# The opening of an attention-and-experts kernel: rest rows loaded per head pair, one load order over two queues, own buffers per pair, seven first banks

## The chip, the cores and the metric

The kernel runs on one core of one Trainium2 chip. The metric is the device time of one execution in microseconds (us); the value of a kernel is the median of its runs. Five engines work side by side, each through its own queue in order: PE (TensorE, matrix products and transposes), ACT (ScalarE: exp, relu, copies), DVE (VectorE: elementwise work), POOL (GpSimd) and SP (SyncE), the last two mostly issuing loads and stores. An engine whose next instruction waits holds up everything behind it. PSUM is the matrix results' memory, eight banks of 128 x 512 fp32.

## What is computed

```python
def phi(x):
    return np.where(x > 0, x, np.exp(x) - 1.0) + 1.0
q_p, k_p = (phi(q), phi(k))                      # q, k, v: 8 batches, 8 heads, 576 rows, 64
kv = np.einsum('bhsd,bhse->bhde', k_p, v)
z = np.sum(k_p, axis=2)
num = np.einsum('bhsd,bhde->bhse', q_p, kv)
den = np.einsum('bhsd,bhd->bhs', q_p, z)[..., None] + 1e-06
attn = num / den                                 # -> x: 4608 rows, 512 columns
p = domain_probs / (domain_probs.sum(-1, keepdims=True) + 1e-09)
for e in range(E):                               # 4 experts, w1 512 x 1024, w2 1024 x 512
    h = np.maximum(x @ w1[e], 0.0)
    out += p[:, e:e + 1] * (h @ w2[e])
```

Linear attention per head, then a mixture of four two-layer experts with the weights p.

## The kernel before

Each batch of 576 rows is cut into 512 main rows (NT) and 64 *rest rows* (R). The 512 columns of x are four head pairs of 128 columns (pr = 0 to 3; also the four pieces dc of the first layer's contraction). The kernel goes through three stages.

*Opening.* Batch 0 goes through attention on PE with transposes done by PE, in `attention(..., two=True)`: exp of k and q on ACT (L472), phi on DVE (L456, L457), transposes of q (L484), kv products (L515, L517, L523), copies of kv and of transposed q on ACT (L534, L535, L497), numerator and denominator (L548, L550), division on DVE (L555, L556), and `turn_x`, which transposes x back (L671) and copies it into xt0 (L676). Then expert 0 runs on x of batch 0: `first_l1` (matmuls L681, relu L713 on ACT) and `first_l2` (L691; sum on DVE, L748 and L750), followed by experts 1 to 3 on the same rows. Attention of batch 1 (kv products L520 and L523, transposes L484 and L489, numerators L571) is woven in between. Where PE would stand idle early, `keep_warm` puts in matmuls whose result nobody reads (L1075).

*Steady part.* From about 81 us, 64 units (`l1_seven` L835, `l2_unit` L911) run a seven-product scheme over the remaining row blocks and experts, with sums of weights that DVE forms beforehand (`sums_w1` L633, `sums_w2` L654; buffers w1x and t123), and attention of batches 2 to 7 with transposes by DMA.

*End.* The last unit's sums and stores.

The order on each queue comes from a planner written into the kernel (`Plan`): every operation is added with engine, estimated duration, priority and the keys that it reads and writes; `lay_out` places the operations in time, `deadlines` sets the priority of all but PE's work to the latest time that PE's plan allows, and a second `lay_out` gives the order in which they are issued. POOL's queue keeps the order in which operations were added. T0 is the planned time of the first unit, TU the planned length of one; WARM and COLD set where filler matmuls are put.

Loads (`dma`, all at L262) go through SP's queue or POOL's. POOL's loads can convert fp32 to fp16 on the way. POOL waits for the landing of the load eight before it in its own row, so that at most eight are under way. In the opening, `load_pair` brings k, q, v of a head pair (main rows, 256 KB each; v through POOL in fp16), `load_rest` the 64 rest rows of all heads of k, v or q (128 KB, runs of 256 bytes, over 64 partitions). The order before: SP: k0, rest k, q0, rest v, v0. POOL, from the landing of k0 on (hold="k0"): k1 q1 v1, k2 q2 v2, k3 q3 v3, the four pieces of w1 of expert 0, probabilities, four pieces of w2 of expert 0, rest q, w1 and w2 of expert 1, then k, v, q of batch 1's first pair and its rest rows, weights of expert 2, and so on.

Pair 3 reuses the load buffers of pair 0; kqp, ek and the transpose bank (l2b1) alternate over two or are shared. The rest rows' phi and the cast of v run over all heads at once (L379, L382, L374, L375) and every kv product ends with one matmul over them (L523). `first_l1(0, ..., 4)` starts four of the eight column blocks (fj) of the first layer in four PSUM banks, dc by dc; the others follow in three banks, four matmuls each.

Of the kernel before, what the change touches and what calls it, by code (L numbers as in the profile page):

```python
# [20 lines left out]
class Plan:  # L21
# [13 lines left out]
    def __init__(self):  # L35
        self.ops = []
        self.wr = {}
        self.rd = {}

    def add(self, eng, dur, pri, fn, r=(), w=(), move=0.0, after=0.0, lead=1.2):  # L40
        n = len(self.ops)
        deps = set()
        for key in r:
            if key in self.wr:
                deps.add(self.wr[key])
            self.rd.setdefault(key, []).append(n)
# [12 lines left out]
    def deadlines(self):  # L59
# [10 lines left out]
        for n, o in enumerate(ops):  # L70
            if o["eng"] != "PE" and o["pri"] >= -99:
                o["pri"] = late[n]
# [61 lines left out]
def kernel(  # L134
# [27 lines left out]
    WARM, COLD = 22.0, 28  # L162
    T0, TU = 79.0, 6.4
# [7 lines left out]
    def sb(name, shape, dt):  # L171
# [47 lines left out]
    v00 = vss[1].rearrange("p h c d -> p (h c d)").bitcast(FP16)[:, 2 * C * D :].rearrange(  # L219
        "p (h c d) -> p h c d", h=2, c=C  # L220
    )
    ones = sb("ones", [P, 2, 1], FP16)
    rc4 = sb("rc4", [P, 2 * C], FP32)
# [20 lines left out]
    def lk(i):  # L244

        return ("l2b2k", "l2b2n") if i == 2 else ("l2b%d" % i,)

    def stage_keys(i):

        if i < 2:  # L250
            return ("st", i, 0), ("st", i, 1), ("st", i, 2)
        return ("xp", 0), ("xp", 1), ("u2", 0)
# [35 lines left out]
    def v16(i):  # L288

        flat = vss[i].rearrange("p h c d -> p (h c d)").bitcast(FP16)  # L290
        return flat[:, 0 : 2 * C * D].rearrange("p (h c d) -> p h c d", h=2, c=C)

    def load_pair(b, pr, queue, pri, after=0.0, hold=None):
        hs = slice(2 * pr, 2 * pr + 2)
        n = 3 if b < 2 else 2
        i = rot("stage%d" % n, n) if n == 2 else rot("stage3", 3)
        stage[b, pr] = i
        kk = stage_keys(i)
        vo = vss[i] if b or queue == "SP" else v16(i)
        parts = [(k, kqs[i][:, 0], kk[0]), (v, vo, kk[2]), (q, kqs[i][:, 1], kk[1])]  # L300
        if b == 0:
            parts[1:] = parts[:0:-1]
        for t, o, key in parts:
            if (b, pr, key) == (0, 0, kk[1]):
                load_rest(0, "SP", 0, parts=(0,))
            keys = (key, "v00") if (b, key) == (1, ("st", 1, 2)) else (key,)
            dma(queue, pri, o, t[b, hs, 0:NT].rearrange("h (p c) d -> p h c d", c=C), keys,
                0.7,
                hold="w" if b == 2 else hold if key == kk[0] else None,
                mark="k0" if (b, pr, key) == (0, 0, kk[0]) else None, after=after)  # L310

    def load_rest(b, queue, pri, after=0.0, parts=(0, 1, 2)):
        par = b % 2
        rs = slice(par * R, par * R + R)
        for i in parts:
            t, o = ((k, kqr[rs, 0]), (v, vr[rs]), (q, kqr[rs, 1]))[i]
            dma(queue, pri, o, t[b, :, NT:S].rearrange("h s d -> s h d"), (("str", par, i),),
                1.1,
                hold="w" if b in (2, 3) else None, after=after)
# [26 lines left out]
    def probs(b0, b1, raw, keys, out_key, pri):  # L346
# [7 lines left out]
            r=keys, w=(out_key,))  # L354
# [10 lines left out]
    def rest_maps(b, pe_mode, pri, parts=(0, 1)):  # L365
# [19 lines left out]
        if not pe_mode:  # L385
            pl.add("SP", 1.25, pri + 1, lambda: nc.sync.dma_start_transpose(
                out=qTr[par][:, :, rs], in_=kqpr[rs, 1].rearrange("p h d -> p (h d)")),
                r=("qpr",), w=[("qTr", par, i) for i in range(DC)], move=0.9, lead=0.2)

# [44 lines left out]
    def attention(b, pr, pe_mode, pri, step, two=False):  # L434
# [16 lines left out]
        zi = pr if two else rot("kvz", 2)  # L451
# [8 lines left out]
        if two:  # L460
            vh = v00 if pr == 0 else v16(si)
            vk = "v00" if pr == 0 else sk[2]

        def vcast():
            if two:
                nc.scalar.copy(vh, vs)
            else:
                nc.scalar.copy(vp[:, :, :, 0:D].rearrange("p c h d -> p h c d"), vs)

        order_ = (0, 1)  # L470
        for i in order_:
# [4 lines left out]
            if i == 0 and not (two and pr):  # L476
                pl.add("ACT", 0.52, pri + step, vcast, r=(sk[2],), w=(vk,))
        if pe_mode:

            tq, tk = (l2b[1].bitcast(FP16), "l2b1") if two else (tbank, "l2b3")  # L480

            def turn():
# [4 lines left out]
                if two:  # L487
                    return
# [7 lines left out]
                   r=(("kqp", pi, 1), "ident") + (() if two else ("qpr",)), w=(tk,))  # L496
            pl.add("ACT", 0.5, pri + 3.5 * step, lambda: nc.scalar.copy(  # L497
                qT.rearrange("p c t -> p (c t)"), tq[:, 0:NT]), r=(tk,), w=(("qT", ti),))
            if not two:
                pl.add("DVE", 0.2, pri + 3.5 * step, lambda: nc.vector.tensor_copy(  # L500
                    qTr[par][:, pr, rs], tq[:, NT : NT + R]), r=(tk,), w=(("qTr", par, pr),))
# [6 lines left out]
        if two:  # L508
            kvs_, kvk = l2b[2][:, 0 : 2 * DE], ("l2b2k",)
        kv3 = kvs_.rearrange("p (h e) -> p h e", h=2)  # L510

        def kv():
            for c in range(C):
                if two:
                    nc.tensor.matmul(out=kv3[:, :, 0:D], lhsT=kp[:, c], rhs=vh[:, :, c],  # L515
                                     start=(c == 0), stop=False, skip_group_check=True)
                    nc.tensor.matmul(out=kv3[:, :, D:DE], lhsT=kp[:, c], rhs=ones,  # L517
                                     start=False, stop=False, skip_group_check=True)
                else:
                    nc.tensor.matmul(  # L520
                        out=kvs_, lhsT=kp[:, c], rhs=vp[:, c], start=(c == 0), stop=False
                    )
# [6 lines left out]
                skip_group_check=two,  # L529
# [7 lines left out]
        pl.add("PE", 0.42 if two else 0.3, pri + 4 * step, kv,  # L537
# [4 lines left out]

        if two:
            den = l2b[2][:, 256 : 256 + 2 * C].rearrange("p (c h) -> p c h", h=2)

            def nd0():
                for c in range(C):
# [590 lines left out]
```

## Time and profile before

| | |
|---|---|
| median of 10 runs | 498.7 us (498.3 to 499.67) |
| profiled execution | 499.45 us, of which the span from first to last instruction is 497.2 |
| mean granted clock of PE | 0.999 |
| DMA traffic | 67.11 MB, 135 GB/s in the mean; read from HBM 45.16 MB |
| chain that ended last | PE 88%, DMA 6%, ACT 2% |
| costliest lines | L835 and L911, the two layers of the steady part: 40% and 38% of the chain |

Read it so: PE is busy nearly from end to end, and the chain that ended last runs through PE for most of the span; the rest of that chain lies in the opening.

Landings that the text uses (issue by the timeline, plus time to landing from the view of DMA issues):

| load | issued | landed |
|---|---|---|
| k0 (SP) | 0.74 | 3.7 |
| v3 (POOL) | 9.95 | 14.75 |
| w1 of expert 0, first piece | 10.66 | 17.2 |
| probabilities, 16 KB | 12.78 | 22.3 |
| w1 of expert 1, last piece | 23.72 | 32.6 |
| batch 1, first pair: k, v, q | 29.46, 30.66, 31.92 | 39.3, 40.5, 41.5 |

### The profile page before, as it was taken

The numbers are of one execution on the slowest core, as the hardware profiler recorded it, in microseconds if no ns is written. First come the engines' busy times: TensorE is split into PE (matmuls) and PEld (weight loads), VectorE is DVE, ScalarE is ACT, GpSimd is POOL, SyncE is SP. The second block draws the span as 40 slices with busy tenths as digits, with TensorE's granted clock in tenths as the row PEclk, the third lists the DMA queues.
The fourth block names the chain that finished last, engine by engine and source line by source line (L and its number), as shares of the span: only waits on it lengthen the run. The fifth ranks groups of instructions, "written<-read, shape, count | busy, mean of one in ns | idle before, by whom it ended". The sixth has DMA issues, their size and how long they took to land.

```text
span 497.2 us, 15010 instructions
## 1 busy us (share of the span) xinstructions
PE 486.2 (98%) x6109; PEld 431.0 (87%) x6109; DVE 408.9 (82%) x1033; ACT 366.5 (74%) x690; POOL 41.6 (8%) x67
## 2 busy tenths in 40 slices
PE   7899999999999999999999999999999999999995
PEld 5644456999999999999999999999999999999995
DVE  5688998988998999899988899889988675767664
ACT  5637758978987798769876988689766767676641
POOL 7566700000000000000000000000000000000000
PEclk9999999999999999999999999999999999999999
DMA  8999979846674774775755755755623333423211
GB/s 228 197 235 213 264 153 212 198 108 171 124 167 120 165 175 125 124 176 118 167 130 158 146 149 123 172 136 121 161 54 86 35 97 44 77 54 86 45 44 42
DMA packets 125573, 67.11 MB, mean 135 GB/s; under 512 B 95520, under 2 KB 119600, under 8 KB 125504
## 3 DMA queue, kind: packets, MB, share of 16 engines
q1 hardware_dynamic: 116112, 51.79, 47.1%
q0 software_dynamic: 9232, 14.10, 13.8%
q8 instruction: 47, 0.77, 0.6%
q10 hardware_dynamic: 160, 0.26, 0.1%
q14 instruction: 22, 0.18, 0.1%
HBM read 45.16 MB, written 9.44 MB: 110 GB/s over the span
## 4 chain that ended last, share of the span: by engine, by line
PE 88%; DMA 6%; ACT 2%; DVE 1%; POOL 1%; issue 1%; SPq 0%; DVEq 0%; POOLq 0%
PE l1b L835 40%; PE l2b L911 38%; PE l2b L691 4%; PE l1b L681 3%; DMA w<-in_moe_w_dram 3%; DMA vs<-in_v_dram 2%; PE at L571 2%; PE at L520 1%; DMA kq<-in_q_dram 1%; ACT xp L795 0%; DVE ot L975 0%; DVE w1x L633 0%; ACT h L849 0%; POOL kq L262 0%; PE at L523 0%
## 5 line engine op out<-in xcount | busy, mean ns | idle before, releaser
L835 PEld LDWEIGHTS <-w 128*128 128x128 f16 x2048 | 133.4, 98 | 5.2
L849 ACT ACTIVATE h<-l1b 128x512 f16<-128x512 f32 x128 | 76.8, 600 | 53.8 <-PE l1b L835 48.8
L911 PE MATMUL l2b<-w,h 128*128 128x256 f16 x768 | 114.9, 273 | 0.0
L911 PE MATMUL l2b<-t,s 128*128 128x256 f16 x768 | 114.4, 273 | 0.0
L835 PEld LDWEIGHTS <-w1x 128*128 128x128 f16 x1536 | 100.1, 98 | 3.9 <-issue 0.2
L911 PEld LDWEIGHTS <-s 128*128 128x128 f16 x1024 | 90.8, 98 | 6.6
L855 DVE CUSTOM_DVE_ANT_0 h<-l1b,p 128x512 f16<-128x512 f32 x64 | 44.2, 690 | 45.9 <-PE l1b L835 42.7
L795 ACT ACTIVATE xp<-x,p_nat 128x512 f16<-128x512 f16 x112 | 77.5, 721 | 0.9 <-DVE x L584 0.5
L835 PE MATMUL l1b<-xT,w 128*128 128x128 f16 x1024 | 78.1, 219 | 0.0
L835 PE MATMUL l1b<-xs,w 128*128 128x128 f16 x1024 | 78.1, 219 | 0.0
L835 PE MATMUL l1b<-xs,w1x 128*128 128x128 f16 x1024 | 77.9, 219 | 0.1
L911 PEld LDWEIGHTS <-h 128*128 128x128 f16 x768 | 67.4, 98 | 4.5
L897 DVE TENSOR_TENSOR s<-h 128x512 f16<-128x512 f16 x128 | 53.9, 421 | 2.1
L852 ACT COPY l1b<-l1b 128x512 f32<-128x512 f32 x64 | 36.7, 574 | 12.2 <-PE l1b L835 11.5
L852 ACT COPY u<-l1b 128x512 f32<-128x512 f32 x64 | 37.4, 585 | 11.1 <-PE l1b L835 10.9
L855 DVE CUSTOM_DVE_ANT_0 h<-l1b,u 128x512 f16<-128x512 f32 x64 | 43.8, 685 | 1.1 <-PE l1b L835 0.4
L852 ACT COPY p<-l1b 128x512 f32<-128x512 f32 x64 | 37.3, 583 | 8.9 <-PE l1b L835 7.2
L472 ACT ACTIVATE ek<-kq 128x512 f16<-128x512 f32 x60 | 37.9, 632 | 3.6 <-DMA kq<-in_k_dram 2.7
L813 DVE TENSOR_TENSOR xs<-xT,xs 128x256 f16<-128x256 f16 x128 | 36.9, 288 | 3.4
L835 PE MATMUL l1b<-xT,w1x 128*128 128x128 f16 x512 | 39.0, 219 | 0.0
L911 PE MATMUL l2b<-w,s 128*128 128x256 f16 x256 | 38.4, 273 | 0.0
L457 DVE TENSOR_TENSOR kqp<-ek,kqp 128x512 f16<-128x512 f16 x64 | 27.2, 425 | 6.1 <-ACT ek L472 1.8
(128 smaller groups left out, 579.1 us busy)
## 6 DMA issues: line engine op xcount, KB each, us to landing
w<-in_moe_w_dram POOLq DMA_DIRECT2D x32, 256.0 KB, 8.0
out_dram<-ot SPq DMA_DIRECT2D x16, 512.0 KB, 3.2
kq<-in_k_dram SPq DMA_DIRECT2D x25, 256.0 KB, 3.2
kq<-in_q_dram SPq DMA_DIRECT2D x25, 256.0 KB, 3.7
vs<-in_v_dram SPq DMA_DIRECT2D x25, 256.0 KB, 3.7
kq<-in_k_dram POOLq DMA_DIRECT2D x5, 256.0 KB, 7.2
kq<-in_q_dram POOLq DMA_DIRECT2D x5, 256.0 KB, 6.1
xT<-xp SPq DMA_TRANSPOSE x64, 3.1
```

Of the source, the lines that this page charges most:

```text
L457: nc.vector.tensor_tensor(out=o, in0=ek[:, i], in1=o, op=AO.min)
L472: pl.add("ACT", 0.55, pri + i * step, lambda i=i: nc.scalar.activation(ek[:, i], kq[:, i], AF.Exp), r=(sk[i],), w=(("ek", ei, i),))
L681: nc.tensor.matmul(out=bank, lhsT=w1_sb[e][:, dc, fj * P : (fj + 1) * P], rhs=xt0[:, dc, :], start=(dc == 0), stop=(dc == DC - 1),)
L691: nc.tensor.matmul(out=bank, lhsT=hts[ht[fj]][:, c * P : (c + 1) * P], rhs=w2_sb[e][:, fj, :], start=(fj == 0), stop=(fj == FC - 1),)
L795: pl.add("ACT", 0.6, pri, lambda c=c, src=src, ps=ps: nc.scalar.activation(xp[:, c, :], src, AF.Copy, scale=ps), r=r, w=(("xp", xi, c),))
L813: lambda o=o, a=a, b_=b_: tt(out=o, in0=a, in1=b_, op=AO.subtract),
L835: nc.tensor.matmul(out=bank[:, fc * P : (fc + 1) * P], lhsT=wt[:, kc, fc * P : (fc + 1) * P], rhs=r[:, kc, :], start=(start and fc == 0 an ...
L849: return lambda: nc.scalar.activation(o, bank, AF.Relu)
L852: return lambda: nc.scalar.copy(o, bank)
L855: return lambda: nc.vector._custom_dve(TENSOR_ADD_SAT, out=o, in0=bank, in1=t, s0=BIG, s1=0.0)
L897: pl.add("DVE", 0.36, U(n + 1) + d - 0.5, lambda i=i, a=a, b_=b_, alu=alu: tt(out=s4[:, i], in0=a, in1=b_, op=alu), r=r, w=(Q(i),))
L911: nc.tensor.matmul(out=l2b[bank][:, half * HD : (half + 1) * HD], lhsT=a[:, c, :], rhs=w[:, c], start=(opens and first and c == 0), stop=( ...
```

## The change

Batch 0's attention gets functions of its own, and the old `two` branch of `attention` and `turn_x` go.

- **Loads.** `load_first` loads one of k, q, v of a pair; each pair has its own buffers, laid into memory that experts 2 and 3 need later (w1x, t123; the planner learns of it through `alias`). All four v come through POOL in fp16. `load_first_rest` loads the rest rows of k or v one head pair at a time: 32 KB, over 32 partitions, runs of 512 bytes, in place of 128 KB over 64. The new order: SP: k0, q0, k1, rest k of pairs 2 and 3, q1, rest v of pairs 0 to 3. ACT: rest k of pairs 0 and 1. POOL: v0, k2, q2, v1, first piece of w1 of expert 0, k3, q3, v2, v3, then the other three pieces, probabilities, w2 and so on as before. Rest q is loaded as before.
- **Rest rows.** `first_rest` does exp, phi and the cast over 128 x 256 elements; each kv product now ends with two pairs of matmuls over 32 partitions (rows of one head pair) in place of one over 128.
- **PSUM.** Numerators use two banks in turn (at, l2b1), transposes of q two halves of l2b3, transposes of x a part of l2b2. The last pair runs in two halves from phi(q) on.
- **First layer.** Seven column blocks start at once (l1b0, l1b1, l2b0, at, l2b3, l2b1, l1b2); the last piece dc=3 is done in two halves; relu of blocks 0, 2, 4, 6 goes to DVE.
- **Elsewhere.** Constants T0 79 to 77, WARM 22 to 21; filler matmuls write l1b2 and stop where the first layer first uses it; some DVE work may not start before 22 in the plan; w1 of expert 3 is loaded in one piece ahead of the last pair of batch 1. As a result of the new plan, all 32 second-layer matmuls of expert 0 stand ahead of expert 1 on PE (24 before), and on ACT the cast of v of batch 1's first pair (after: L602) stands behind that pair's relus, rest exps and rest cast, where before it stood between exp of k and exp of q.

```diff
-    WARM, COLD = 22.0, 28
-    T0, TU = 79.0, 6.4
+    WARM, COLD = 21.0, 28
+    LATE, RELU = 0.5, (0, 2, 4, 6)
+    T0, TU = 77.0, 6.4
...
+    def load_first(queue, pri, t, pr, hold=None, mark=None):
+        if t is v:
+            o, key = v_o[pr], ("v_o", pr)
+        else:
+            o, key = kqs[pr][:, int(t is q)], stage_keys(pr)[int(t is q)]
+        dma(queue, pri, o, t[0, 2 * pr : 2 * pr + 2, 0:NT].rearrange("h (p c) d -> p h c d", c=C),
+            (key,), 0.72, hold=hold, mark=mark)
+
+    def load_first_rest(t, o, queue, pri, key, g):
+
+        n = 2 * R // DC
+        dma(queue, pri, o[g * n : (g + 1) * n].rearrange("p h t d -> p h (t d)"),
+            t[0, 2 * g : 2 * g + 2, NT:S].rearrange("h (p t) d -> p h (t d)", t=2),
+            ((key, g),), 0.17)
...
+    def first_rest():
+        o = kp_r.rearrange("p t h d -> p h t d")
+
+        def maps():
+            nc.vector.tensor_scalar(o, k_r, 0.0, 1.0, AO.max, AO.add)
+            nc.vector.tensor_tensor(out=o, in0=ek_r, in1=o, op=AO.min)
+
+        pl.add("ACT", 0.36, 3, lambda: nc.scalar.activation(ek_r, k_r, AF.Exp),
+               r=[("k_r", g) for g in range(DC)], w=("ek_r",))
+        pl.add("ACT", 0.36, 4, lambda: nc.scalar.copy(v_r, v_r32),
+               r=[("v_r32", g) for g in range(DC)], w=("v_r",))
+        pl.add("DVE", 0.6, 3.5, maps, r=[("k_r", g) for g in range(DC)] + ["ek_r"], w=("kp_r",))
...
+    def first_attention(pr, pri, step):
...
+        ek, kqp, vh, kvz, qT = ek_o[pr], kqp_o[pr], v_o[pr], kvs[pr], qT_b[pr % 2]
...
+        def kv():
+            parts = [(kqp[:, 0, c], vh[:, :, c], ones) for c in range(C)]
+            parts += [(kp_r[g, t], v_r[g, :, t], ones[g]) for t in range(2)]
+            for i, (kk, vv, oo) in enumerate(parts):
+                for o, x in ((kv3[:, :, 0:D], vv), (kv3[:, :, D:DE], oo)):
+                    nc.tensor.matmul(out=o, lhsT=kk, rhs=x, start=(i == 0 and x is vv),
+                                     stop=(i == len(parts) - 1), skip_group_check=True)
...
+        parts = 2 if pr == DC - 1 else 1
...
     def first_l1(e, pri, step, nb):
         ht = []
         banks = [(l1b[i], "l1b%d" % i) for i in range(3)]
-        if nb == 4:
-            banks += [(l2b[0], "l2b0")]
+        if nb > 3:
+            banks[2:] = [(l2b[0], "l2b0"), (at, "at"), (l2b[3], "l2b3"), (l2b[1], "l2b1")]
+            banks += [(l1b[2], "l1b2")]
...
+            if nb > 3 and fj in RELU:
+                pl.add("DVE", 0.62, pr_, lambda: nc.vector.tensor_scalar(
+                    hts[ht[fj]], bank, 0.0, None, AO.max), r=(key,), w=(HTK[ht[fj]],))
+                return
...
+            late = lambda fj: LATE if fj > 2 else 0.0
+            for dc, u in [(dc, 2) for dc in range(DC - 1)] + [(DC - 1, 0), (DC - 1, 1)]:
+                ts = slice(0, NT) if u == 2 else slice(u * NT // 2, (u + 1) * NT // 2)
...
-    load_pair(0, 0, "SP", 0)
-    load_rest(0, "SP", 0, parts=(1,))
-    load_pair(0, 1, "POOL", 0, hold="k0")
-    load_pair(0, 2, "POOL", 0)
-    rest_maps(0, True, 3, (0,))
+    load_first("SP", -9, k, 0, mark="k0")
+    load_first("SP", -8, q, 0)
+    load_first("SP", -7, k, 1)
+    for g in range(DC):
+        load_first_rest(k, k_r, "ACT" if g < 2 else "SP", -6, "k_r", g)
+    load_first("SP", -5, q, 1)
+    for g in range(DC):
+        load_first_rest(v, v_r32, "SP", -4, "v_r32", g)
+    load_first("POOL", 0, v, 0, hold="k0")
+    for pr in (2, 3):
+        load_first("POOL", 0, k, pr)
+        load_first("POOL", 0, q, pr)
+        if pr == 2:
+            load_first("POOL", 0, v, 1)
+            load_w1(0, (0,))
+    load_first("POOL", 0, v, 2)
+    load_first("POOL", 0, v, 3)
+    first_rest()
     for pr in range(DC):
-        if pr == 3:
-            load_pair(0, 3, "POOL", 0)
-            load_w1(0, range(DC))
-            probs(0, 2, p5_b, ("p5",), "pnat0", 24)
-            load_w2(0)
-            load_rest(0, "POOL", 0, parts=(2,))
-        attention(0, pr, True, 2.5 + pr, 0.4, two=True)
-        turn_x(pr, 4.9 + pr)
+        first_attention(pr, 2.5 + pr, 0.4)
+    load_w1(0, range(1, DC))
...
-    ht = first_l1(0, 17.5, 0.1, 4)
+    ht = first_l1(0, 17.5, 0.1, 7)
...
+    load_w1(3, (2, 3))
     load_pair(1, 3, "POOL", 0)
-    load_w1(3, (2, 3))
     load_w2(3)
...
+        warm = True
         for o in todo:
-            if o["eng"] == "PE" and o["start"] < WARM:
+            warm = warm and "l1b2" not in o["w"] and o["start"] < WARM
+            if o["eng"] == "PE" and warm:
```

## The prediction

> **What bounds the kernel now.** I read the page first: TensorE (PE) is busy for 98% of the span, so only the places where it isn't can give anything back.
>
> ```profile
> span 497.2 us, 15010 instructions
> PE 486.2 (98%) x6109; PEld 431.0 (87%) x6109; DVE 408.9 (82%) x1033; ACT 366.5 (74%) x690; POOL 41.6 (8%) x67
> ```
>
> "Busy" counts keep_warm too, the filler matmuls of L1075, so the second view is PE's own timeline around the place where filler ends and real work becomes dense.
>
> ```profile
> 22.17 0.39 PE L671 MATMUL l2b<-s,x 128*128 128x128 f16 x4
> 22.39 1.04 PE L1075 MATMUL l2b<-qTr,s 128*128 128x256 f16 x8
> 23.26 0.81 PE L681 MATMUL l1b<-s,w 128*128 128x512 f16 x3
> 24.34 3.62 PE L681 MATMUL l1b<-s,w 128*128 128x512 f16 x16
> 27.80 1.46 PE L691 MATMUL l2b<-w,h 128*128 128x512 f16 x6
> ```
>
> Read: the last pair's x is transposed at 22.17, filler runs, and from 23.26 twenty first-layer matmuls (0.216 us apart) of expert 0 still stand ahead of its second layer at 27.80. From there PE waits once, for 0.26 us. So all that a change of the opening can win lies before 27.80, and PE's order behind it keeps the gain only if nothing else makes PE wait.
>
> The third view tells who would. The chain of waits leaves PE at 41.72 and goes back through ACT into the load stream:
>
> ```profile
> 30.66 9.88 DMA vs<-in_v_dram
> 40.54 0.02 issue
> 40.56 0.02 ACT vp L468
> 40.58 0.50 issue
> 41.09 0.60 ACT h L713
> 41.68 0.04 issue
> 41.72 1.02 PE l1b L681 x4
> ```
>
> ACT works in order. It waited for k of batch 1's first pair, then for v (landed 30.66 + 9.88 = 40.54); a relu stood behind that, and PE behind the relu. The stream is full all along: one table of stretches gives the DMA share (second number from the right), short only before 4 us.
>
> ```profile
> 2.00:3.00 1.00, 0.45 (x3) 0.33 (x3) 0.91 (x8) 0.02 (x1) 0.00 (x0) 1.00 0.68 234
> 3.00:4.00 1.00, 1.00 (x7) 0.69 (x6) 0.82 (x4) 0.25 (x1) 0.00 (x0) 1.00 0.74 141
> 30.00:42.00 12.00, 11.74 (x61) 5.30 (x60) 8.79 (x17) 4.35 (x8) 5.85 (x10) 1.00 1.14 218
> ```
>
> Below, ACT's own timeline at that place, and from the view of DMA issues (size, us from issue to landing) the load of q that the first line waits for: issued 31.92, so landed at 41.5.
>
> ```profile
> 41.60 0.63 ACT L472 ACTIVATE ek<-kq 128x512 f16<-128x512 f32 x1
> 42.13 0.58 ACT L713 ACTIVATE h<-l1b 128x512 f16<-128x512 f32 x1
> 42.73 0.63 ACT L379 ACTIVATE ek<-kqr 64x512 f16<-64x512 f32 x1
> 43.39 1.08 ACT L713 ACTIVATE h<-l1b 128x512 f16<-128x512 f32 x2
> 44.50 0.62 ACT L382 CAST vpr<-vr 64x512 f16<-64x512 f32 x1
> 45.02 0.62 ACT L379 ACTIVATE ek<-kqr 64x512 f16<-64x512 f32 x1
> ```
>
> ```profile
> kq<-in_q_dram POOLq DMA_DIRECT2D x1, 256.0 KB, 9.6
> ```
>
> **Part 1: the front of the opening (PE's own path).** Own buffers per pair remove the wait of one pair for another's kqp, ek and transpose bank. The changed program's PE order shows what seven banks do: when the last quarter of w1 (dc=3) is needed, 19 full-width matmuls' worth stand ahead of the second layer (8 of the middle quarters, the 7 last ones in halves, 4 of the eighth bank), since three of the banks are still in attention's use until late; before it was 20. So the banks alone give 0.2 us. What counts is when these matmuls start. Before, x's last copy ended 22.59 + 0.58 = 23.17; dc=3 had landed at 22.1 (fourth of the issues from 10.66, 9.8 us). After, the x chain is no longer late: ACT's whole list up to the last x copy is 8 exps of 0.63, the two quarter-size pieces at 0.36 or so (half of 0.63 rounded up), 4 qT copies of 0.58, 4 kvz of 0.42, 4 x copies of 0.58: 5.0 + 0.7 + 2.3 + 1.7 + 2.3 = 12.0 us from 3.75, with some 4 us of waits for k2, k3 and norms, about 20. But in PE's order the last pair's x transposes stand behind a dc=2 matmul, and dc=2 landed at 20.9. So the start is set by the weights, at 22.1 less what the stream gains. First layer ends at 22.1 − s + 19 x 0.216 = 26.2 − s, against 27.80: PE is 1.6 + s ahead, s being how much earlier the stream runs. The four relus moved to DVE (0.62-0.69 each) fall where DVE idles (3.1 us busy of 6 in 18 to 24); without that cover they would cost their sum, 2.6. The casts of v0 and the 64-partition casts that vanish take 1.2 us off ACT, which waits there anyway. Behind it the planner now puts all 32 second-layer matmuls ahead of expert 1 (24 before); that is 8 x 0.216 = 1.7 us of cover for w1 of expert 1, last landing 23.72 + 8.9 = 32.6. Expert 1 would start at 26.2 − s + 6.9 = 33.1 − s, just behind 32.6 − s: no stall. Halves of the last pair add a few small instructions, hidden in the same wait for weights.
>
> **Part 2: the stream (s).** POOL's nine pair loads become eight: k1 and q1 go to SP, v0 comes. Pair loads land from 4.03 + 4.6 = 8.6 to 9.95 + 4.8 = 14.75, eight steps of 0.77. One step fewer: 0.77. The bytes stay the same, so if the engines are the limit it is 0, the lower end. Then the engines' idle share before 4 us, 0.32 + 0.26 = 0.58: the queue starts with k0, q0, k1 in place of a 128 KB load of 256-byte runs, and I take half, 0.3 (0 to 0.58). Rest rows: two loads of 128 KB become eight of 32 KB. Rows: behind q of batch 1 three 128 KB rest loads landed at 41.9, 42.6, 43.3, that is 0.6 each, 1.2 for two. The smallest loads of the trace (16 KB, 4 KB) landed 0.15 to 0.2 behind the one ahead. Eight at 0.15 make 1.2: nothing won or lost, my value, as 32 KB is nearer to these. At 0.6 each they would be 4.8, a loss of 3.6. The two loads that ACT issues now cost it about 0.6 each (SP's issues: 0.46 to 0.75); its table load (1.28) then ends at 3.2, still before k0 lands at 3.7. POOL's hold on k0 is unchanged; what is queued behind it moves as summed. SP's last four rest loads wait for semaphores of loads that land before 7: nobody but the v cast waits for them. s = 0.77 + 0.3 + 0 = 1.1, bounds −3.6 and 1.4 (to 2.5 if the lag of the slowest engine is not there: w1's dc=2 landed 2.4 after dc=1, while the steady step is 1.3, from 13.50 + 9.9 to 17.51 + 9.8 in three steps).
>
> [...]
>
> **Part 3: where the front's gain meets the stream.** The changed ACT order behind q of batch 1's first pair is: exp q, relu, exp rest k, two relus, cast rest v, exp rest q, and only then the cast of v, which came before all these until now. By the rows shown: 0.09 + 0.63 + 0.58 + 0.63 + 1.08 + 0.62 + 0.62 + 0.63 = 4.9, less about 0.1 of overlap, 4.8. PE's first batch-1 matmul (L520, at 46.04 before, 4.5 behind q's landing) needs that cast, so it starts at 41.5 − s + 4.8 = 46.3 − s. PE itself would be there at 46.04 − 0.26 − 1.6 − s = 44.2 − s and waits some 2 us in pieces: at the eighth bank (relu behind exp k), at the second half of the second layer, at the cast. So the gain is not 1.9 + s but s − 0.27 = 0.83. Queued behind the cast on ACT are kvz and qT of that pair, which PE needs 2 us later.
>
> **The rest.** The third expert's w1 is not late: landed by 40.82 + 6.9 = 47.7, used at 50.53. Moving w1 of expert 3 (two loads, 2.6 us) ahead of the last pair delays that pair to about 62.6 − s; ACT idles 3.4 us up to 67.36 there. Without that cover it would cost up to 2.6. Fewer filler matmuls: PE idled over 0.6 us before 17.35 with clock 1.00. The steady part is PE from end to end, and keeps what it is handed.
>
> **Sum.** The profiled execution took 499.45 (span 497.2 and 2.25 around it); it becomes 498.6. Runs have median 498.7, 0.75 under it; the difference carried over: 498.7 − 0.8 = 497.9.
>
> **Rivals.**
> - *The front's whole gain arrives* (chance 0.20): loads of batch 1 land over 2 us earlier than I think, the lag of the slowest engine being absent, so ACT's queue holds nobody. For: the lag began at single weight loads (2.4 against 1.3). Against: it was still there at 41.5. 1.6 + 1.1 = 2.7, 496.0 (495.6 to 496.8).
> - *The transfer was hidden anyway* (0.13): the stream is bound by bytes, s = 0, and the v cast's new place costs its 0.27: 499.0 (498.6 to 499.8). For: share over 1 from 4 us on. Against: the idle before 4 us.
> - *Small loads are dear* (0.17, the slower side): each of the eight takes the engines as long as a 128 KB one, in the first 8 us, and everything behind lands later. At 0.6 each s = 1.1 − 3.6 = −2.5 and the time 501.5. It makes the kernel slower from 0.25 each on (8 x 0.25 = 1.2 + 0.83), by over 0.2% from 0.38. For: 128 KB loads cost 0.6 whatever they hold. Against: the 4 and 16 KB rows.
>
> **Numbers.** My case has 0.50, its own range 497.0 to 498.8. About 0.2% (1.0 us) is what runs of this kernel can tell from no change: faster is under 497.7, slower over 499.7. Faster: 0.21 of my case and the first rival, 0.41. Same: 0.29 and 0.10 of the second, 0.39. Slower: 0.17 and 0.03, 0.20. The range 495.9 to 499.9 leaves out about 0.07 below and 0.13 above.
>
> **What would show it.** First layer of expert 0 ending near 25.1 (26.2 − s), second layer at once behind it; q of batch 1's first pair landing near 40.4; PE waiting about 2 us in all between 36 and 45, for ACT; first batch-1 matmul near 45.2. Wrong, if PE waits nowhere there, if the first layer is late while its weights have landed, or if rest rows land after 9 us and the first kv waits for them.

## The result, and the profile after

The changed kernel takes 503.47 us in the median (500.75 to 504.65 over nine runs) against 498.6 (497.72 to 499.97) for the kernel before, measured side by side: a ratio of 1.0088, 95% interval 1.0075 to 1.01. It is 0.9% slower. The forecast was 497.9 us, range 495.9 to 499.9.

The profiled execution of the changed kernel took 502.54. Its page, the lines that answer to the first ones shown of before:

```profile
span 500.4 us, 15033 instructions
PE 487.2 (97%) x6111; PEld 431.2 (86%) x6111; DVE 412.4 (82%) x1041; ACT 363.5 (73%) x687; POOL 41.0 (8%) x66
...
PEclk9899999999999999999999999999999999999999
```

The span grew by 3.2 us, PE's busy time by 1.0; so PE idles 2.2 us more. The last row is the granted clock in 40 slices of 12.5 us: its second digit, an 8, stands where before had a 9. PE's own timeline, at the place where 22.17 to 27.80 was shown of before (start, duration, line, idle before it in brackets):

```profile
25.91 0.27 PE L532 MATMUL l2b<-s,x 128*128 128x128 f16 x2
26.02 0.38 PE L761 MATMUL l2b<-s,w 128*128 128x512 f16 x1
26.23 0.27 PE L761 MATMUL l1b<-s,w 128*128 128x256 f16 x1
...
30.35 7.07 PE L772 MATMUL l2b<-w,h 128*128 128x512 f16 x32
```

The last x is transposed at 25.91 (22.17 before) and the second layer of expert 0 starts at 30.35 (27.80 before; 25.1 forecast). That 2.55 us is what arrives at the end: the last group of matmuls starts at 493.85 instead of 491.25. Another 0.6 us lies behind PE's last group (500.4 − 493.85 = 6.55, before 497.2 − 491.25 = 5.95); I have no cause for it; e1, which keeps the plan, has it too (6.61), e2 to e9 do not (5.90 to 6.09).

So the loss is in the front. Which waits? PE's waits by what released them (us in all, times, longest), the longer ones of the changed kernel, then the longest of the kernel before; both also have one of 2.5 us ahead of the first filler:

```profile
PE l2b L532 <- DVE t L493: 2.0, 1, 2.0
PE l2b L506 <- ACT s L571: 1.1, 2, 0.7
PE l2b L517 <- ACT s L571: 0.6, 1, 0.6
```

```profile
PE l2b L1075 <- ACT qT L497: 2.6, 3, 1.2
```

Before, PE's front waits came in pieces of at most 1.2 us with filler between. Now one piece is 2.0 us long, 13.78 to 15.78, ahead of the first transposes of x (L532). The chain that ended last, cut at 20 us, goes through that place:

```profile
7.71 6.91 DMA w1x<-in_k_dram
14.62 0.02 issue
14.64 0.64 ACT t L549
15.28 0.02 issue
15.30 0.44 DVE t L493
15.74 0.04 issue
15.78 0.38 PE l2b L532 x4
...
16.52 0.59 ACT s L571
17.11 0.04 issue
17.15 0.71 PE l2b L506 x12
17.86 0.94 PE l1b L761 x2
```

k of pair 3 was issued at 7.71 and landed 6.91 us later, at 14.62; before, it was there at 12.77. Yet L532 transposes x of pair **0**, which has nothing to do with pair 3's k. ACT's timeline shows the link:

```profile
11.71 0.21 ACT L511 CAST kvz<-l2b 64x65 f16<-64x65 f32 x1
14.64 0.63 ACT L549 ACTIVATE t<-w1x 128x512 f16<-128x512 f32 x1 [2.72 <-DMA w1x<-in_k_dram]
15.30 0.21 ACT L510 CAST kvz<-l2b 64x65 f16<-64x65 f32 x1
15.52 0.21 ACT L511 CAST kvz<-l2b 64x65 f16<-64x65 f32 x1
...
16.52 0.58 ACT L571 COPY s<-l2b 128x512 f16<-128x512 f16 x1
```

ACT works in order. It stood 2.72 us before pair 3's exponential (L549), and behind that the two copies of kv of pair 1 (L510, L511), whose products were ready at 13.0. Before, pair 1's copies stood ahead of pair 3's exponential:

```profile
13.17 0.21 ACT L534 CAST kvz<-l2b 64x65 f16<-64x65 f32 x1 [0.78 <-DVE rc L555]
...
14.11 0.63 ACT L472 ACTIVATE ek<-kq 128x512 f16<-128x512 f32 x1
```

The copies read PSUM bank l2b2, and the transposed x goes into another part of the same bank. The profile names DVE (L493) as the releaser of L532, but the second copy of kv on ACT ended at the same 15.73, so the profile alone can't tell the two apart. It was not x of pair 0: that was ready at 14.06 (13.37 + 0.69), and PE loaded it (PEld) and then stood:

```profile
14.11 0.10 PEld L532 LDWEIGHTS <-x 128*128 128x128 f16 x1 [0.61 <-DVE x L523]
```

That it was the bank, e3 below shows. The same bank holds the denominators. DVE's reciprocals of pairs 1 and 2:

```profile
17.97 0.21 DVE L522 RECIPROCAL rc<-l2b 128x8 f32<-128x8 f32 x1 [2.24 <-PE l2b L506]
...
21.83 0.21 DVE L522 RECIPROCAL rc<-l2b 128x8 f32<-128x8 f32 x1 [1.86 <-PE l2b L506]
```

Their denominators (L517) were done at 16.5 and 20.2, but the releaser is L506, the kv products of the *next* pair. So kv products wait for the x copy (0.68 us up to 17.15, 0.44 up to 20.84), reciprocals for the kv products (2.24 and 1.86), kv copies on ACT for the reciprocals (0.63 up to 18.21, 1.00 up to 22.07): one bank works off the whole chain in series. The planner keeps the three uses apart under keys of their own (l2b2k, l2b2n, l2b2x), so its plan has none of these waits. No run here shared the bank without these waits.

Last, the clock. A table of three stretches (length, PE busy, granted clock, DMA share, GB/s):

```profile
11.04:14.45 3.41, 2.58 (x35) 1.00 1.00 226
14.45:17.86 3.41, 1.41 (x25) 1.00 1.18 210
17.86:21.28 3.42, 2.98 (x25) 0.50 1.20 206
```

After the stretch with the gap, PE ran 3.42 us at half clock; before, the tables give 1.00 up to the tail. In seven of the ten executions the mean clock was 0.985 to 0.994, lower than the 0.995 of the profiled one (0.999 before), and the time goes with it: 500.75 at 0.997, 504.65 at 0.987.

In this execution the stream, which the forecast was mostly about, came out as forecast. q of batch 1's first pair, issued at 30.15, row of DMA issues:

```profile
kq<-in_q_dram POOLq DMA_DIRECT2D x1, 256.0 KB, 10.3
```

It landed at 40.45 (41.5 before, 40.4 forecast). And the ACT list behind it:

```profile
42.79 0.63 ACT L605 ACTIVATE ek<-kq 128x512 f16<-128x512 f32 x1
...
46.86 0.63 ACT L602 CAST vp<-vs 128x512 f16<-128x512 f32 x1
```

From the exp of q to the end of the cast of v, 4.7 us, as summed (4.8); but both start when ACT comes to them, not when q lands: PE was too late to wait for either.

### The profile page after: what moved, and what is told of

It reads as the page before. It is cut to its first block, busy times and chain, and to the rows that moved or that the text cites. A ratio compares the mean times of both kernels' runs of the same rounds, so it can differ in the third digit from the quotient of the medians.

```text
span 500.4 us, 15033 instructions
## 1 busy us (share of the span) xinstructions
PE 487.2 (97%) x6111; PEld 431.2 (86%) x6111; DVE 412.4 (82%) x1041; ACT 363.5 (73%) x687; POOL 41.0 (8%) x66
## 4 chain that ended last, share of the span: by engine, by line
PE 91%; DVE 2%; DMA 2%; ACT 2%; POOL 1%; issue 1%; DVEq 0%
PE l1b L924 39%; PE l2b L1000 37%; PE l2b L772 6%; PE l1b L761 5%; PE at L664 2%; DMA w1x<-in_k_dram 1%; PE at L640 1%; DMA kq<-in_k_dram 1%; PE l2b L761 1%; DVE ot L1064 0%; DVE h L944 0%; DVE s L986 0%; ACT xp L884 0%; ACT s L571 0%; PE l2b L532 0%
## 5 line engine op out<-in xcount | busy, mean ns | idle before, releaser
L941 ACT COPY u<-l1b 128x512 f32<-128x512 f32 x64 | 37.4, 584 | 11.0 <-PE l1b L924 10.7
L605 ACT ACTIVATE ek<-kq 128x512 f16<-128x512 f32 x54 | 33.8, 629 | 0.1
L986 DVE TENSOR_TENSOR s<-s,h 128x512 f16<-128x512 f16 x64 | 27.2, 425 | 6.1
```

Of the source, the lines that this page charges most:

```text
L605: pl.add("ACT", 0.55, pri + i * step, lambda i=i: nc.scalar.activation(ek[:, i], kq[:, i], AF.Exp), r=(sk[i],), w=(("ek", ei, i),))
L941: return lambda: nc.scalar.copy(o, bank)
L986: pl.add("DVE", 0.36, U(n + 1) + d - 0.5, lambda i=i, a=a, b_=b_, alu=alu: tt(out=s4[:, i], in0=a, in1=b_, op=alu), r=r, w=(Q(i),))
```

## The experiments

Three suspects in series, then: the load of k of pair 3 (late behind the first piece of w1), ACT's order, the shared bank; and the clock as a fourth, cause or consequence. Each is taken away alone, then together. All ratios are to the kernel before, run beside them; "layer 2" is the start of expert 0's second layer in the profiled execution, a single one: with the same load order (after, e1, e3, e4, e7, e11, e12) k of pair 3 landed anywhere from 13.91 to 14.79, so a few tenths there tell little.

| run | what is changed | median us | ratio (95%) | layer 2 | half clock in the front |
|---|---|---|---|---|---|
| before | | 498.6 to 498.9 | 1 | 27.80 | none |
| after | | 503.47 | 1.0088 (1.0075, 1.01) | 30.35 | 3.4 us |
| e1 | filler in the gap | 501.25 | 1.0043 (1.0028, 1.0058) | 29.45 | none |
| e2 | load order | 500.26 | 1.0027 (1.0017, 1.0038) | 27.42 | none |
| e3 | x in its own bank | 498.77 | 0.9986 (0.9965, 1.0006) | 28.28 | 3.4 |
| e4 | x and den in own banks | 499.03 | 1.0002 (0.9988, 1.0016) | 27.70 | 3.4 |
| e5 | e2 + e4 | 497.99 | 0.9979 (0.9968, 0.999) | 26.53 | 3.4 |
| e6 | e2 + e3 | 498.38 | 0.9995 (0.9983, 1.0006) | 26.81 | none |
| e7 | ACT's order | 499.24 | 1.0014 (1.0003, 1.0025) | 28.04 | none |
| e8 | before without filler | 499.92 | 1.0022 (1.0011, 1.0033) | 29.05 | 10.2 |
| e9 | e5 + filler | 497.74 | 0.9976 (0.9965, 0.9988) | 25.95 | none |
| e10 | e9 + ACT's order at 36 to 45 | 498.88 | 0.9997 (0.9989, 1.0005) | 26.09 | none |
| e11 | four first banks | 503.57 | 1.0088 (1.0064, 1.0111) | 32.09 | 10.2 |
| e12 | e4 + e7 | 499.77 | 1.0015 (1.0003, 1.0027) | 26.53 | none |

**e1, filler in the gap.** Before the planner's own filler, extra dummy matmuls ahead of three named operations:

```diff
+            if o["eng"] == "PE" and o["w"] and o["w"][0] in ("l2b2x", "l2b2k"):
+                seen[o["w"][0]] = seen.get(o["w"][0], -1) + 1
+                for _ in range(MORE.get((o["w"][0], seen[o["w"][0]]), 0)):
+                    keep_warm()
...
+        seen, MORE = {}, {("l2b2x", 0): 16, ("l2b2k", 2): 5, ("l2b2k", 3): 3}
```

> The changed kernel with 24 more dummy matmuls: 16 ahead of the first turn of x (where PE idled 2.00 us from 13.78), 5 ahead of the third pair's kv products (idle 0.68 at 16.5), 3 ahead of the fourth pair's (idle 0.44 at 20.4). Nothing else moves. One dummy took 0.115 to 0.12 us in this trace, so they fill about 1.9, 0.6 and 0.35 us that were idle. Theory A (the idle PE loses its clock): the granted clock stays at 1.00 from 9 to 30 us, the matmuls of 17.8 to 21.3 take 0.216 us again instead of 0.43, which gives back 1 to 1.5 us of the first layer (end 30.5 to about 29.2), and the runs spread less; 500.5 to 502 us against 503.5. Theory B (the chain of x is late by itself, the clock only follows): the clock stays at 1.00 and the time changes by less than 0.5 us, since PE waits for the chain as long as before. If the clock falls all the same, it is not the idle PE that lowers it.

Measured: 501.25 us, clock 1.00 from 9 us to the tail, spread 0.6 us over four runs in place of 3.9 over nine. Theory A. The clock is worth 0.45% (1.0088 to 1.0043), some 2.2 us, more than the 0.9 us by which the two profiles differ (layer 2 at 30.35 and 29.45; in e1's, k of pair 3 also happened to land 0.7 us earlier). Most executions of the changed kernel lose more clock than the profiled one (0.985 to 0.994 in seven of ten, against 0.995). The other half of the loss, 0.43%, stays: PE is as late as the chain makes it.

**e2, load order.**

```diff
             load_first("POOL", 0, v, 1)
-            load_w1(0, (0,))
...
-    load_w1(0, range(1, DC))
+    load_w1(0, range(DC))
```

> The changed kernel with the first piece of the first expert's weights loaded after the last v, not between v of pair 1 and k of pair 3; nothing else. That piece stands for about 1.25 us of the stream (the steps between the next pieces, 17.77, 19.02, 20.30). Theory A (k of pair 3 is late behind that piece, and holds up ACT, which waits 2.72 us for it with the copies of kv of pair 1 queued behind): k of pair 3 lands near 13.3 instead of 14.62, the PE gap of 2.00 us shrinks to about 0.8, the clock stays at or near 1.00, and the first layer ends 1.3 to 2.6 us earlier; 500.5 to 502 us. Theory B (the shared bank sets the pace from pair 1 on): k3 lands earlier but the kv products of pairs 2 and 3 still wait for the copies of x, and no more than the 1.3 us of the load comes back; 502 us or more. Theory C (the loss lies in the clock alone): what counts is only whether the clock falls.

ACT's timeline:

```profile
11.90 1.33 ACT L549 ACTIVATE t<-w1x 128x512 f16<-128x512 f32 x2
13.26 0.21 ACT L510 CAST kvz<-l2b 64x65 f16<-64x65 f32 x1
```

Pair 3's exponentials start at 11.90, 2.74 us earlier than in the changed kernel, twice what was expected, and the copies of kv of pair 1 at 13.26 in place of 15.30. No filler was added, and the clock held. 500.26 us, just under its range: theory A. But kv products still waited for the x copy (0.68 us at 15.35), so the bank is not all innocent.

**e3 and e4, the bank.** e3 moves the transposed x into l1b2 (filler into l1b1, six first banks); e4 moves the denominators into l2b0 as well (five first banks).

```diff
-        xt = l2b[2].bitcast(FP16)[:, NT : 2 * NT]
+        xt = l1b[2].bitcast(FP16)[:, 0:NT]
...
-        d0 = 136 + ni * 2 * C
-        den = l2b[2][:, d0 : d0 + 2 * C].rearrange("p (c h) -> p c h", h=2)
+        den = l2b[0][:, ni * 256 : ni * 256 + 2 * C].rearrange("p (c h) -> p c h", h=2)
```

> The changed kernel with the turned x of the opening in another PSUM bank (the third of layer one, which so leaves the first seven, six are left) and the dummy matmuls in the second bank of layer one. Theory A (one PSUM bank holds kv, the denominators and the turned x, so that each waits for the other): the first turn of x starts near 14.1, as soon as x is normalised, not at 15.78; the kv products of pairs 2 and 3 wait no more for the copies of x (0.68 and 0.44 us); the first layer ends 1.5 to 2.5 us earlier; 500.5 to 502 us. Theory B (the loads set the pace): ACT still waits until 14.64 for k of pair 3, so the copies of kv of pair 1, and with them the products of pair 1, stay at 15.8; under 0.7 us comes back. Six banks in place of seven cost little in either: the seventh's four matmuls are 0.87 us of PE work that lies later.

> As e3_xt, and the denominators in a bank of their own too (the first of layer two; five first banks are left). In the changed kernel's trace the reciprocals at 17.97 and 21.83 waited for the kv products of the next pair (17.72, 21.65), though their own denominators were done at 16.5 and 20.0, and the kv copies on ACT waited for the reciprocals (18.21, 22.07). Theory A (one bank in series): these waits go, up to 1.5 us at each of two pairs; the first layer ends 2.5 to 4 us earlier than 30.5 and so near or before the 27.8 of the kernel before; 499 to 501 us. Theory B (loads and ACT's order set the pace): no more than e3_xt gives. With five banks instead of seven, if the banks matter for covering the end of the chain, it ends up to 0.87 us per bank later than e3_xt.

Measured: 498.77 and 499.03 us. Both give back all of the loss although the load and ACT's wait for it are as late as before. In e3 the first transposes of x start as soon as that x is ready, in place of 15.78, while the copies of kv of pair 1 on ACT (15.41) and DVE's phi (15.42) come as late as in the changed kernel:

```profile
14.49 0.40 PE L533 MATMUL l1b<-s,x 128*128 128x128 f16 x4 [0.33 <-DVE x L524]
```

In e4 the reciprocal of pair 1 no longer waits for the next pair's kv products but for its own denominators (L518):

```profile
16.30 0.21 DVE L523 RECIPROCAL rc<-l2b 128x8 f32<-128x8 f32 x1 [0.66 <-PE l2b L518]
```

Theory A, and more than expected for e3, which stands 1.7 us under its range. e4 wins 0.58 us over e3 in layer 2 but nothing in the median; the intervals overlap, so whether the denominators' own bank is worth anything is not told. The clock fell in both profiles for as long as in that of the changed kernel, so these are not faster by way of the clock. Over all executions they lose less clock (mean 0.994 to 1.000 in e3, 0.993 to 1.000 in e4, against 0.985 to 0.997), so part of what the medians gain is clock all the same.

**e7, ACT's order.** Loads and banks stay; pair 3's two exponentials are put behind what PE needs.

```diff
             pl.add("ACT", 0.62, pri + i * step, lambda i=i: nc.scalar.activation(
-                ek[:, i], kq[:, i], AF.Exp), r=(sk[i],), w=(("ek", pr, i), (("ek", pr, i), 0)))
+                ek[:, i], kq[:, i], AF.Exp), r=(sk[i],), w=(("ek", pr, i), (("ek", pr, i), 0)),
+                after=14.0 if pr == 3 else 0.0)
```

> The changed kernel with its loads and banks as they are, but with pair 3's two exponentials put behind the copies of kv of pair 1 and the copy of x of pair 0 in ACT's list. k of pair 3 lands at 14.6 as before. Theory A (ACT's order: what stands behind the wait for k of pair 3 is what PE needs): the copies of kv of pair 1 run near 13.4, not at 15.30; PE's gap of 2.00 us falls under 1.0; the clock holds; pair 3 is later by 0.5 us or so; 500 to 501.5 us. Theory B (late load): pair 3 comes last anyway and the first layer ends where it did, 30.0 to 30.5; over 502 us, or under that by the clock alone.

```profile
13.26 0.21 ACT L510 CAST kvz<-l2b 64x65 f16<-64x65 f32 x1 [1.45 <-DVE rc L522]
...
15.24 0.63 ACT L549 ACTIVATE t<-w1x 128x512 f16<-128x512 f32 x1
```

499.24 us, 0.8 under its range: putting two exponentials later on ACT, with the load about as late as it was (14.24), takes back 0.74 of the 0.88%; the clock held, which e1 prices at 0.45. (In the new plan DVE's phi of pair 3 moved with them, behind pair 1's division.) Theory A, and theory B is out: pair 3 starts 0.6 us later on ACT than in the changed kernel and the first layer ends 2.3 us earlier. What was late was not pair 3; it was everything behind it in ACT's list.

**e8, the clock by itself.** The kernel before with WARM from 22.0 to 8.0, which drops 35 dummy matmuls.

```diff
-    WARM, COLD = 22.0, 28
+    WARM, COLD = 8.0, 28
```

> The kernel before without the 35 dummy matmuls that it places after 8 us; nothing else moves. It shows the price of the clock by itself. PE then idles some 2 us and more at a time between 9 and 17.4 us, and the chain of x is untouched. Theory A (idle PE lowers the clock): the granted clock is 0.50 for one stretch or more of 3.4 us between 10 and 27, the first layer ends 1 to 2.5 us later than 27.80, and the time is 500 to 502 us against 498.6 to 498.9, with more spread. Theory B (the clock does not hang on these): clock 1.00, no change within 0.3 us.

Its stretches:

```profile
9.06:12.48 3.42, 1.24 (x25) 1.00 1.03 313
12.48:15.89 3.41, 2.91 (x29) 0.50 1.11 159
15.89:19.30 3.41, 2.83 (x24) 0.50 1.08 197
19.30:22.72 3.42, 3.42 (x21) 0.50 1.22 205
```

Half clock for 10.24 us, and yet only 1.25 us later in layer 2 (29.05) and 0.22% slower: theory A, its time just under the 500 given. The last copy of x ends 1.3 us later than before (24.49, before 23.17), and PE goes on with the first layer from there. More spread did not come (499.17 to 500.56).

**e5, e6, e9: the two causes together.** e5 is e2 and e4 in one, e6 is e2 and e3, e9 is e5 with eleven more dummy matmuls (`MORE = {("l2b2k", 0): 3, (("num", 0), 0): 8}`, over all keys).

> e2_order and e4_den together: the first piece of weights loaded after the last v, and turned x and denominators each in a bank of their own. In e4_den PE idled 1.70 us from 13.99 for the copies of kv of pair 1, behind k of pair 3 on ACT, and the clock was 0.50 for 3.41 us from 15.87; in e2_order k of pair 3 landed 2.74 us earlier (11.88) and the clock held. Theory A (two separate causes, the load and the bank, and the clock follows from the gap): no PE gap over 0.8 us after 12, clock 1.00, first layer ends near 26.5 (27.70 of e4_den less about 1.2 for the clock), the last group of matmuls starts near 490.5 against 491.25 of the kernel before; 497.0 to 498.3 us, at or below the kernel before (498.9 with these runs). Theory B (the weights, the last of which land near 20.3, or PE's own work set the end as soon as either cause is gone): no better than the better of the two, 498.8 to 500.

> e2_order and e3_xt together: as e5_den_order, with the denominators left in the bank of kv, so that each reciprocal still waits for the kv products of the next pair. If that wait matters once the load and the x bank are mended, this ends its first layer 0.5 to 1.5 us later than e5_den_order; if it doesn't, both agree within 0.3 us, and six banks in place of five cost or save nothing. 497.3 to 499 us; clock 1.00.

> e5_den_order with 11 more dummy matmuls: 3 ahead of the kv products of pair 0 and 8 ahead of the products of pair 0 (where PE idled 0.42 us at 10.29 and 0.95 at 12.41 before the clock of 0.50 from 13.36 to 16.77). Theory A (idle PE lowers the clock, and what is left of the loss is that): clock 1.00, first layer ends 25.3 to 26.2 against 26.53, 496.8 to 497.9 us against 497.99. Theory B (something else is late next): the clock holds, but PE then waits more at 40.7 for ACT (0.37 us in e5_den_order, behind batch 1's q, which lands at 41.1), as much as the front gained; 497.7 to 498.3.

e5 and e9 beat both kernels: 497.99 and 497.74 us, 0.2% under the kernel before. Theory A of e5 holds for the time, not for the clock: PE's idle pieces were 0.42 and 0.95 us, and half clock came all the same, from 13.36. e9 removes it, and layer 2 starts at 25.95, the earliest of all and 1.85 us ahead of the kernel before. The waits of PE in e9 show what limits it now:

```profile
PE l1b L762 <- DMA w<-in_moe_w_dram: 0.7, 1, 0.7
PE l1b L762 <- ACT h L800: 0.3, 1, 0.3
```

the first piece of weights (moved back), and ACT at 40.11. e9 and e5 can't be told apart by their intervals, nor e6 from e5. e6 starts layer 2 0.28 us after e5, within the 0.3 that its forecast gave for "it doesn't matter"; but its clock held and e5's did not, so what a bank for the denominators is worth stays open.

**e10 and e12: does the front's gain arrive?** e10 is e9 with later earliest times in ACT's plan for batch 1's first pair and rest rows, so that expert 1's relus go ahead; e12 is e4 with the order of e7.

```diff
-                ek[:, i], kq[:, i], AF.Exp), r=(sk[i],), w=(("ek", ei, i),))
+                ek[:, i], kq[:, i], AF.Exp), r=(sk[i],), w=(("ek", ei, i),),
+                after=(36.5, 39.2)[i] if (b, pr) == (1, 0) else 0.0)
...
+                       after=37.6 if (b, pr) == (1, 0) else 0.0)
...
+                after=40.2 + i if b == 1 else 0.0)
...
+                       after=40.7 if b == 1 else 0.0)
```

> e9_den_order_fill with ACT's list round 36 to 45 us changed: the relu evictions of expert 1 stand ahead of the exponentials and casts that wait for batch 1's late loads, but one. If theory B of e9_den_order_fill holds, PE's wait of 0.37 us or more at 40.7 goes or halves, and this is 0.3 to 0.8 us under e9; if the front's gain comes through there without it, both agree within 0.3 us. A new wait can come later: the kv products of batch 1's first pair start up to 1 us later when their cast and exponential do.

> e4_den (own banks, loads as in the changed kernel) with ACT's order of e7_act: pair 3's exponentials behind the copies of kv of pair 1 and of x of pair 0. If ACT's order, not the time at which k of pair 3 lands, is what made e4_den idle 1.70 us at 13.99, that idle falls under 0.8, the clock holds, and the time is that of e5_den_order, 497.5 to 498.5 us, though k of pair 3 still lands at 14.6. If the late load itself sets the end once the banks are apart, the first layer ends 0.5 to 1.5 us after e5_den_order's 26.53, and the time is 498.5 to 499.5.

e12's front is as early as e5's (26.53 both) and its clock held, with k of pair 3 landing at 13.96: so ACT's order, not the landing, made e4 idle. But its time is 1.8 us longer than e5's. Neither theory of it foresaw where that goes:

```profile
PE l1b L763 <- ACT h L801: 1.2, 2, 0.7
```

PE waits 0.51 and 0.71 us at 39.84 and 41.58 for relus that stand behind batch 1's loads on ACT: the very mechanism of the forecast's Part 3, seen only when the front is early. More idle pieces follow (0.44 us between 80 and 90), not all of them traced. In e10 this wait is gone, and still the kernel is 1.1 us slower than e9, against an expectation of 0.3 to 0.8 faster. Its PE table has a hole that e9 (20.00 of 20 there) has not:

```profile
110.00:130.00 20.00, 19.74 (x270) 1.00 0.66 164
```

One piece of it is a wait of 0.21 us at 127.05 for a copy on ACT (L946). It explains little: of the 1.2 us between the two profiles, 0.14 is there at layer 2, 0.73 comes between layer 2 and PE's last group of matmuls, and 0.33 behind that group. The cause was not pursued; this stays open.

**e11, the seven banks.** `first_l1(0, 17.5, 0.1, 4)` in place of 7.

> The changed kernel with four first banks for the first layer instead of seven; loads, pairs and banks of the opening are as they are. With four, the matmuls of three of the first three quarters (3 x 3 of 0.216 us, 1.9 us in all) can't run while x is late and come after its end. Theory A (the banks cover part of the late chain): the first layer ends 1 to 1.9 us later than 30.4; 504.5 to 505.5 us. Theory B (with the chain as it is, PE has other work or the clock decides): within 0.5 us of 503.5.

503.57 us, ratio 1.0088, the same as with seven: theory B by the time, though these are four runs, and the interval ends just short of theory A's 504.5. Its profiled execution has layer 2 at 32.09, but with 10.2 us of half clock, so its front can't be set against that of the other one.

## Why the prediction was wrong

- **Part 1, "the x chain is no longer late" and "about 20" for ACT's last x copy: this is the step that failed.** The last copy started at 26.2. I gave ACT 12.0 us of work and "some 4 us of waits"; from 3.89 to its end it took 22.7, so the waits were nearer 10.7. Two things were left out. The change gives each pair its own SBUF buffers, but x, kv and the denominators share one PSUM bank; I had listed that bank in the change and counted the removed waits only. kv and the denominators shared l2b2 before, too (L509, L544); new is the transposed x, which used to go to l2b3 (L675). e3, which takes x alone out again, shows the price: all of the loss. And ACT's new list has pair 3's exponential ahead of pair 1's kv copies, the other way round from before, which I could have read off, as I did in Part 3 for the cast of v; e7 shows it: 0.74 of 0.88%. With the chain late, the weights (issued from 10.57 on, 7.8 us each) no longer set the start of anything: the last piece was there near 20.3 and the first layer ended at 30.35, one of the prediction's own signs of being wrong.
- **Parts 1 and 2 gave no price of its own to k of pair 3 going behind a piece of weights.** For the stream as a whole it is neutral; for k it meant landing at 14.62 in place of 12.77 (8.47 + 4.3). e2 shows what hangs on it. The three causes do not add up: each single removal brings back 0.6% or more, as they stand in one chain, and breaking it anywhere lets PE go on.
- **"PE idled over 0.6 us before 17.35 with clock 1.00", so fewer fillers cost nothing: wrong.** e1 puts the clock at 0.45%, half of the loss, and e8 shows that the kernel before needs its fillers too (0.22%).
- **Part 2, s = 1.1: met in this execution, but not shown.** q landed 1.05 us earlier. Yet e8, which has the loads of the kernel before, had it at 40.14, and the seven kernels with the new load order at 39.71 to 40.63: the gain is no larger than what executions differ by, and its parts (0.77, 0.3, 0) were not taken apart. From these landings it can be said that the eight 32 KB loads did not cost the stream several us; and the last of the eight was issued by SP at about 5.2 and took 3.5 us, so it was there by 8.7, before the 9 that would have proved it wrong. The rival "small loads are dear", 3.6 us dearer at 0.6 each, is not borne out; no run undid these loads alone. The kernel came out on that rival's side all the same, by another way. No view shows the "slowest engine" that the upper bound and the first rival name; what the traces have is a step of 2.4 us between two landings of w1 before, and steps of 1.25 and 1.28 in the changed kernel (17.77, 19.02, 20.30).
- **Part 3** (PE waits for ACT between 36 and 45; first batch-1 matmul at 45.2): not reached. PE waited nowhere there and the matmul came at 48.17, pushed by the front. The list's length was right, and e12, e5 and e9 show the wait (1.2, 0.4, 0.3 us) once the front is early, smaller than the 2 us given.
- **"The steady part keeps what it is handed"** holds for the loss (2.55 us at 30.35, 2.6 at the end). It does not for every gain: from the start of layer 2 to PE's last group of matmuls the kernel before took 463.45 us and the changed one 463.50, but e5 464.52, e10 464.59 and e12 465.79.

## What to carry to other kernels

When a change gives stages their own buffers, list every resource that they still share, PSUM banks above all, and ask of each engine's in-order list what stands *behind* an instruction that will wait for a load: the late load hurt here through pair 1's copies queued behind it, and these through the bank that tied pair 0's x to them. PE's 2.0 us gap cost twice here, by the wait and by the 3.4 us at half clock that followed; such a gap can be filled (e1, 0.45% back), or the chain that makes it broken (e2 and e7, whose profiles kept full clock in the front). And where several causes stand in one chain, removing any one may look like the whole explanation: remove them singly and together before sharing out the loss.

## What the runs showed of the hardware

The granted clock fell in a pattern that can be read from the tables: in the front, half clock came in pieces of 3.41 us (changed kernel, e3, e4, e5) or 10.24, three times that (e8, e11). In the changed kernel the pieces start at 17.86 and, in the tail, at 499.14, 481.28 us apart, which is 141 beats of 3.413, a third of 10.24. Cutting each trace on its own beat, what went with it was PE's busy time in the beat before, not the longest gap. Beats that were followed by half clock, of the changed kernel's variants e5 and e3:

```profile
9.95:13.36 3.41, 2.12 (x31) 1.00 1.13 249
```

```profile
14.80:18.21 3.41, 2.11 (x28) 1.00 1.17 211
```

and two that were not, of e6 and e2:

```profile
8.58:12.00 3.42, 2.14 (x24) 1.00 1.09 285
```

```profile
18.00:21.41 3.41, 2.15 (x23) 1.00 1.21 204
```

In the fourteen profiles all beats of the front with up to 2.12 us busy (1.24 in e8, 1.41 in the changed kernel, 1.54 in e11, 1.72 in e4, 2.11 in e3, 2.12 in e5) were followed by half clock, and none with 2.14 or more, as long as the clock was full. That is 62% busy, by spans whose ends are modelled, and six cases. Left out is the beat in which PE starts, at 2.55 us (0.80 to 4.21 in the changed kernel, 1.66 us busy): the tables print 1.00 there and in the next one too, but the dummy matmuls ran at about half pace, 0.218 us each against 0.119:

```profile
2.55 5.24 PE L1174 MATMUL l1b<-qTr,s 128*128 128x256 f16 x24 [2.55 <-DVE qTr L1098]
...
7.85 1.91 PE L1174 MATMUL l1b<-qTr,s 128*128 128x256 f16 x16
```

So 1.00 is not to be relied on before 7.6 us in that trace. e5's longest idle piece in its beat was 0.95 us; the kernel before survived one of 1.22, its beat being 2.21 us busy. How long half clock lasts I can't say: one beat in the changed kernel, e3, e4 and e5, three in e8 and e11, though the first half-clock beat was much alike, 2.98 us busy in the changed kernel, 2.91 and 3.04 in the other two. The beat did not start with the kernel: counted back from the first half clock, it begins 0.80 us into the span in the changed kernel, 1.14 in e3, 2.24 in e8, 3.12 in e5. So the same gap would fall into it differently in each execution, which fits the changed kernel's spread (500.75 to 504.65); that was not tried by itself.
